# Fixed sizes in place of switches for the experts' second blocks, and a copy moved from GpSimd to ScalarE

## The chip, the cores and the metric

The kernel runs on one core of a Trainium2 chip. The metric is device time in microseconds from the launch to the last output. The core has TensorE (matrix products; PE in the rows, its weight loads PEld), VectorE (DVE), ScalarE (ACT), GpSimd (POOL), and SyncE (SP), which issues most transfers. The engines run side by side, each through its own list of instructions in order, and wait for each other through semaphores. SBUF is the on-chip memory, PSUM the banks that TensorE writes.

## What is computed

The reference chains three layers: a sparse attention over 2 x 768 positions, a routed mixture of eight experts, and a dense layer with a rational activation. The part that the change touches is the second one and the weights of the third:

```python
skip_score = x @ w_skip                       # x: 1536 x 512
xc = x[skip_score > 0]
logits = xc @ w_gate                          # 8 experts
e_idx = np.argmax(logits, axis=1)
for e in range(8):
    mask = e_idx == e
    h = np.maximum(xc[mask] @ w1[e], 0.0)     # 512 -> 1024
    y[mask] = gate_w[mask, None] * (h @ w2[e])
out[do_compute] = xc + y
...
h = x @ w_in                                  # 512 -> 2048
g = P(h) / (Q(h) + 1e-06)                     # P cubic, Q quadratic in |h|
return g @ w_out
```

How many rows an expert gets depends on the inputs. The inputs of the runs are drawn once and stay the same.

## The kernel before

**Attention, routing (up to 96 us).** The attention runs on all engines, and the weights of the first experts are loaded meanwhile. Rows are then sorted by expert: `off` and `end` are an expert's first place and the place behind its last one in the sorted order, `cnt` the difference. `lim` holds the bounds of each block of an expert, `regs` and `pick` hold numbers that engines load into registers.

**Experts (96 to 245 us).** Sorted rows are gathered from DRAM by GpSimd (line 764, `xg`), transposed by TensorE (`turned`, line 1032) and kept as `xs`, rows along the free dimension. An expert's rows are done in two blocks. The first block has up to 32 rows (`SMALL`): `take_first` (VectorE masks and copies the rows into `xw`, lines 864 to 873), `first` (hidden product `th`, line 810), `turn` (`tt`), `parts` (second product `tp`, line 833), `total_first` (`ty`) and `add_first` (VectorE adds the result into `xs`). The second block, the "rest", takes what is left over. Experts 3 to 7 are first reordered by `choose` so that the largest of them stands in slot 3 (`STAY`); only slots 0 to 3 have a rest, and a loop behind `tc.If(left > 0)` (line 1152) takes anything beyond it.

A rest has one of eleven sizes (`ARMS`: 0, 32, 64, 112, 128, 144, 152, 160, 176, 192, 224). VectorE counts which size an expert needs, TensorE and ScalarE load that index (`arms_of`), and `rest` is a `tc.Switch` over eleven written-out arms, with a hint set ahead of it; a switch parts the instruction lists of all engines into blocks. `take_rest` always masks 224 rows (`CAP`), `room` zeroes the whole PSUM tile `py` (line 970), and `update(CAP, ...)` adds 224 columns. The arm of 32 uses the same form as a first block (`thr`, `ttr`, `tpr`, `py`), the arm of 0 nothing, the others `large`: hidden product `phr` (line 783), ScalarE's ReLU `hTr`, second product `py` (line 789).

The weights of experts 3 to 7 are fetched by SyncE (`fetched`, line 1014) into the slots of earlier experts, two matrices of 2 MB each, as soon as TensorE is done with the slot. The order of the whole stage is written out by hand; `turned(4..11)` and `choose` stand behind `rest(0)`; `rest(1)` stands behind `add_first(0)`, `rest(2)` behind `add_first(2)`, `rest(3)` behind `add_first(3)`.

**Decoder.** The dense layer's weights arrive as 64-bit numbers in pieces of 128 x 512. A piece takes three VectorE steps (lines 719, 723, 725, into `dec`, three buffers), then a rounded part `hi` (line 737) and a difference `lo = dec - hi` (line 739). The steps are strewn between the other work by `decoder.steps(fetches, splits)`; half of the 32 pieces are split in the expert stage, half in the last one.

**Dense layer (from 245 us).** 48 rounds, one per 512 rows and 128 hidden units. In each round: product `m` (line 1225), ScalarE's front (lines 1232 to 1234), GpSimd's multiplication `t` (line 1235), ScalarE's logarithm and exponential of the round before (lines 1248, 1249), VectorE's lines 1239 and 1243 and its four steps 1263 to 1268 (`gh`, `u`, `t`, `gl`), and product `z` (line 1283) of two rounds before. Up to three decode steps and three split steps follow VectorE's stages in a round. `split` chooses the engine of `hi`:

```python
if self.on_scalar:
    nc.scalar.activation(hi, src, AF.Copy)
else:
    nc.gpsimd.tensor_scalar(hi, src, 1.0, 0.0, ALU.mult, ALU.add)
yield
nc.gpsimd.tensor_tensor(lo, src, hi.bitcast(F32), ALU.subtract)
```

Of the kernel before, what the change touches and what calls it, by code (L numbers as in the profile page):

```python
# [27 lines left out]
E = 8  # L28
# [41 lines left out]
ARMS = (0, 32, 64, 112, 128, 144, 152, 160, 176, 192, 224)  # L70
# [3 lines left out]
def shape_constants():  # L74
# [27 lines left out]
    ints[:, 305:315] = np.add(ARMS[:-1], 0.5)  # L102
    ints[:, 316:572] = np.arange(256)
    ints[:, 572:604] = np.tile(np.eye(32), (4, 1))
    ints[:, 604:614] = np.add(ARMS[:-1], 0.5)
# [4 lines left out]
def tile_kernel(ctx, tc, q, k, v, w_skip, w_gate, w1, w2, w_in, w_out, pa, pb, ma_d, ints_d, out):  # L110
# [48 lines left out]
    def attention(c, io, wk, ps_s, ps_q, ps_t, ps_o):  # L159
# [468 lines left out]
        for n in range(3):  # L628
# [13 lines left out]
        flag = const.tile([P, E, len(ARMS) - 1], F32, name="flag")  # L642
        nc.vector.tensor_copy(rf[:, 0:9], pb_)
        off, end = rf[:, 0:8], rf[:, 1:9]
        cnt, arm, win, most, fst, sec = (rf[:, 16 + 8 * i : 24 + 8 * i] for i in range(6))
# [3 lines left out]
        nc.vector.tensor_scalar(win, sec, float(N - CAP), None, ALU.min)  # L649
# [4 lines left out]
        nc.vector.tensor_tensor(  # L654
            flag[:],
            lim[:, 3, :, None].to_broadcast(flag.shape),
            ints[:, None, 305:315].to_broadcast(flag.shape),
            ALU.is_gt,
        )
        nc.vector.tensor_tensor(lim[:, 1, :], end, fst, ALU.subtract)  # L660
        nc.vector.tensor_reduce(arm, flag[:], AX.X, ALU.add)
        nc.vector.tensor_tensor(lim[:, 2, :], sec, win, ALU.subtract)
        nc.vector.tensor_copy(regs[:, 8:16], arm[0:1])
        nc.vector.tensor_copy(regs[:, 0:8], win[0:1])
        nc.vector.tensor_copy(regs[:, 40:48], fst[0:1])
        routed.extend([(off, end, cnt), rf[:, 24:40]])
# [91 lines left out]
    with ExitStack() as s_:  # L758
# [97 lines left out]
        def reg(eng, i, top):  # L856
            return eng.value_load(i if not isinstance(i, int) else regs[:, i : i + 1], min_val=0, max_val=top)
# [23 lines left out]
        arms = {}  # L881

        def arms_of(e, which):


            engs = {ET.PE: nc.tensor, ET.Activation: nc.scalar}
            index = {et: reg(eng, which, len(ARMS) - 1) for et, eng in engs.items()}
            arms[e] = index, tc.switch_hint(index, len(ARMS), f"rest{e}")

        def choose():  # L890
# [7 lines left out]
            def t_(name, shape, dt=F32):  # L898
# [4 lines left out]
            left, flag2, win = t_("left", [E]), t_("flag2", [len(ARMS) - 1]), t_("winx", [1])  # L903
# [24 lines left out]
            nc.vector.tensor_scalar(win[:], off2[:, 0:1], float(SMALL), float(N - CAP), ALU.add, ALU.min)  # L928
# [9 lines left out]
            nc.vector.tensor_scalar(more[:, :STAY], off[:, :STAY], float(SMALL + CAP), None, ALU.add)  # L938
            nc.vector.tensor_scalar(more[:, late], off2, float(SMALL), None, ALU.add)
            nc.vector.tensor_scalar(  # L940
                more[:, STAY : STAY + 1], more[:, STAY : STAY + 1], float(CAP), None, ALU.add
            )
# [10 lines left out]
        small, xr, py_first, py_rest, off_first, off_rest = [], {}, {}, {}, {}, {}  # L953
# [22 lines left out]
        def rest(e):  # L976
            a, b_ = wts[e, 1], wts[e, 2]
            py = py_rest[e]
            index, hint = arms[e]
            for i in tc.Switch(index, len(ARMS), hint=hint):  # L980
                n = ARMS[i]
                if n == SMALL:
                    sm = Small(a, b_, xr[e], f"r{e}", ps_h)
                    for step in (sm.hidden, sm.turn, sm.parts):
                        step()
                    sm.total(py, 2)
                elif n:
                    large(a, b_, n, xr[e], py, f"r{e}_{i}")
            update(CAP, off_rest[e], py)
# [60 lines left out]
        with tc.manual_schedule(engines={ET.PE, ET.Activation, ET.DVE, ET.Pool, ET.SP}):  # L1050
# [11 lines left out]
            arms_of(0, 8)  # L1062
            first(0)
            take_rest(0)
            room(0)
# [6 lines left out]
            rest(0)  # L1072
            room(1)
# [21 lines left out]
            arms_of(1, 9)  # L1095
# [9 lines left out]
            room(2)  # L1105
# [4 lines left out]
            arms_of(2, 10)  # L1110
# [11 lines left out]
            room(3)  # L1122
            take_rest(3)
            fetched(5, 4)
            arms_of(3, pick[:, 0:1])
# [64 lines left out]
    with ExitStack() as s_:  # L1190
# [214 lines left out]
```

## Time and profile before

| | value |
|---|---|
| time, median of 3 runs | 557.14 us (554.82 to 558.86) |
| profiled execution | 556.66 us, span 554.9 us |
| busy: TensorE | 466.9 us (84% of the span) |
| busy: VectorE | 409.5 us (74%) |
| busy: ScalarE | 238.6 us (43%) |
| busy: GpSimd | 198.3 us (36%) |
| mean granted TensorE clock | 0.932 of full speed |

The shares are means over stages with different limits, so they name no bound by themselves. The expert stage lies between 96 and 245 us, the dense layer behind it. In the rows below an engine's idle time stands in brackets with what ended it; "issue" means that the engine waited for nothing that the profile shows.

### The profile page before, as it was taken

The page shows a single profiled execution, that of the slowest core. Times are in us where ns is not written, and L with a number is a line of the kernel's source. Part 1 is how long each engine was busy: PE and PEld are TensorE (multiplying, and loading weights), DVE is VectorE, ACT ScalarE, POOL GpSimd, SP SyncE. Part 2 cuts the span into 40 slices and gives each one's busy share as a digit, 9 for nine tenths or more (in the row PEclk, how much of TensorE's full clock was granted, in tenths as well). Part 3 has the DMA queues.
Part 4 walks back from the last instruction along what each step waited for, and adds up shares of the span by engine and source line. Part 5 has one row for each costly group of instructions (what it writes and reads, how often), then busy time and mean ns, then how long its engine had stood idle before and what let it go on. Part 6 is the DMA issues. An engine that isn't in the chain of part 4 may idle for free.

```text
span 554.9 us, 8712 instructions
## 1 busy us (share of the span) xinstructions
PE 466.9 (84%) x3127; PEld 348.3 (63%) x3127; DVE 409.5 (74%) x879; ACT 238.6 (43%) x455; POOL 198.3 (36%) x192
## 2 busy tenths in 40 slices
PE   8999998567868655787977787888999999999994
PEld 4677675344828422345756666567888887888872
DVE  4687678445984231858999999998787797887784
ACT  3565553131112010126444444626565676465650
POOL 2644400710345001635544444644322243322222
PEclk9999998678979887958999999989999999999998
DMA  9799971686393899222222222101000000100001
GB/s 288 219 370 353 402 234 73 183 284 217 133 342 107 292 322 377 85 80 76 76 76 77 76 77 76 38 2 58 20 0 1 0 2 38 38 1 0 2 0 76
DMA packets 28781, 71.67 MB, mean 129 GB/s; under 512 B 3040, under 2 KB 7072, under 8 KB 28704
## 3 DMA queue, kind: packets, MB, share of 16 engines
q1 hardware_dynamic: 24192, 55.26, 28.3%
q0 software_dynamic: 4368, 15.21, 8.1%
q8 instruction: 37, 0.61, 0.4%
q14 instruction: 40, 0.33, 0.2%
q10 hardware_dynamic: 144, 0.27, 0.1%
HBM read 64.44 MB, written 6.29 MB: 127 GB/s over the span
## 4 chain that ended last, share of the span: by engine, by line
PE 18%; DVE 17%; issue 13%; POOL 5%; ACT 2%; POOLq 0%; DVEq 0%; ACTq 0%
PE m L1225 10%; PE z L1283 8%; POOL t L1235 3%; DVE u L1264 2%; DVE t L1267 2%; DVE gh L1263 2%; DVE decwo L719 2%; DVE t L1239 2%; DVE decwi L719 2%; DVE decwi L723 1%; POOL out_dram L1308 1%; DVE decwo L725 1%; DVE gl L1268 1%; DVE decwo L723 1%; DVE decwi L725 1%
## 5 line engine op out<-in xcount | busy, mean ns | idle before, releaser
L1225 PE MATMUL m<-x,wi 128*128 128x512 f32 x576 | 146.2, 405 | 28.5 <-DVE gl L1268 25.9
L1225 PEld LDWEIGHTS m<-x,wi 128*128 128x128 f32 x576 | 110.5, 195 | 59.2 <-DVE gl L1268 29.7
L1235 POOL TENSOR_TENSOR t<-s,t 128x512 f32<-128x512 f32 x48 | 63.3, 1318 | 171.2 <-ACT s L1234 167.8
L1283 PE MATMUL z<-wo,gh 128*128 128x512 f32 x384 | 96.1, 389 | 0.0
L1232 ACT ACTIVATE t<-m,ab 128x512 f32<-128x512 f32 x48 | 37.4, 780 | 113.3 <-PE m L1225 113.3
L1283 PEld LDWEIGHTS z<-wo,gh 128*128 128x128 f32 x384 | 71.9, 188 | 15.2 <-POOL wo L739 0.3
L1283 PE MATMUL z<-wo,gl 128*128 128x512 f32 x192 | 52.6, 391 | 1.1 <-DVE gl L1268 1.1
L1263 DVE SCALAR_TENSOR_TENSOR gh<-t,ab,m 128x512 fp32r<-128x512 f32 (+1 forms) x51 | 36.4, 713 | 17.1 <-ACT m L1249 17.0
L1264 DVE SCALAR_TENSOR_TENSOR u<-t,c,gh 128x512 f32<-128x512 f32 (+1 forms) x51 | 39.3, 770 | 5.5 <-DVE gh L1263 0.5
L1283 PEld LDWEIGHTS z<-wo,gl 128*128 128x128 f32 x192 | 36.0, 188 | 9.8 <-DVE gl L1268 2.3
L1234 ACT ACTIVATE s<-t,absb 128x512 f32<-128x512 f32 x48 | 39.1, 815 | 4.4
L810 PE MATMUL th<-w,xw 128*32 128x256 f32 x256 | 24.2, 548 | 19.3 <-issue 11.1
L1267 DVE SCALAR_TENSOR_TENSOR t<-t,ab,u 128x512 f32<-128x512 f32 (+1 forms) x51 | 36.5, 716 | 1.8
L1239 DVE TENSOR_TENSOR t<-t,m 128x512 f32<-128x512 f32 x48 | 32.8, 684 | 6.1 <-ACT t L1233 5.1
L1268 DVE TENSOR_TENSOR gl<-t,m 128x512 fp32r<-128x512 f32 (+1 forms) x51 | 33.5, 656 | 4.8
L1243 DVE SCALAR_TENSOR_TENSOR t<-t,ab,m 128x512 f32<-128x512 f32 x48 | 35.8, 746 | 1.2
L299 ACT ACTIVATE tm<-tm,mx 128x120 f32<-128x120 f32 x96 | 29.9, 383 | 10.1 <-DVE mx L283 10.0
L1248 ACT ACTIVATE m<-t,c 128x512 f32<-128x512 f32 x48 | 32.3, 672 | 0.2 <-POOL t L1235 0.2
L810 PEld LDWEIGHTS th<-w,xw 128*32 128x32 f32 x256 | 11.3, 150 | 30.3 <-issue 19.2
L283 DVE CUSTOM_DVE_ANT_0 tm<-s,ma 128x120 f32<-128x120 f32 x96 | 21.3, 278 | 11.7 <-PE s L269 11.7
L1249 ACT ACTIVATE m<-m 128x512 f32<-128x512 f32 x48 | 27.9, 582 | 1.5
L1233 ACT ACTIVATE t<-m 128x512 f32<-128x512 f32 x48 | 28.4, 591 | 0.0
(217 smaller groups left out, 728.7 us busy)
## 6 DMA issues: line engine op xcount, KB each, us to landing
w<-in_moe_w_dram SPq DMA_DIRECT2D x16, 2048.0 KB, 11.1
rawwi<-in_moe_w_in_dram POOLq DMA_DIRECT2D x9, 512.0 KB, 4.8
rawwo<-in_moe_w_out_dram POOLq DMA_DIRECT2D x8, 512.0 KB, 4.0
rawwo<-in_moe_w_out_dram SPq DMA_DIRECT2D x8, 512.0 KB, 3.2
rawwi<-in_moe_w_in_dram SPq DMA_DIRECT2D x7, 512.0 KB, 3.5
kT<-in_k_dram SPq DMA_DIRECT2D x8, 400.0 KB, 6.6
ve<-in_v_dram SPq DMA_DIRECT2D x4, 780.0 KB, 7.1
qT<-in_q_dram SPq DMA_DIRECT2D x8, 384.0 KB, 7.9
```

Of the source, the lines that this page charges most:

```text
L810: nc.tensor.matmul(ph[SMALL * g : SMALL * g + SMALL], self.xw[:, c_, :SMALL], self.a[:, c_, 256 * g : 256 * g + 256], start=c_ == 0, stop= ...
L1225: nc.tensor.matmul(ph[:], w[:, l, c_, fs], x[c_][:, r], start=i == 0, stop=i == 3 * KC - 1)
L1232: nc.scalar.activation(t["t2"][:], ph[:], AF.Identity, scale=ab[:, 3:4], bias=ab[:, 2:3])
L1234: nc.scalar.activation(t["s2"][:], t["t1"][:], AF.Identity, scale=absb[:, 1:2], bias=absb[:, 0:1])
L1235: nc.gpsimd.tensor_tensor(t["t1"][:], t["s2"][:], t["t1"][:], ALU.mult)
L1239: nc.vector.tensor_tensor(t["t2"][:], t["t2"][:], ph[:], ALU.mult)
L1243: nc.vector.scalar_tensor_tensor(t["t2"][:], t["t2"][:], ab[:, 1:2], ph[:], ALU.add, ALU.mult)
L1263: nc.vector.scalar_tensor_tensor(gh[:, s], t2[:, s], ab[:, 0:1], r0[:, s], ALU.add, ALU.mult)
L1264: nc.vector.scalar_tensor_tensor(u[:, s], t1[:, s], c1[:, 0:1], gh[:, s].bitcast(F32), ALU.add, ALU.mult)
L1267: nc.vector.scalar_tensor_tensor(t2[:, s], t2[:, s], ab[:, 0:1], u[:, s], ALU.add, ALU.subtract)
L1268: nc.vector.tensor_tensor(gl[:, s], t2[:, s], r0[:, s], ALU.mult)
L1283: nc.tensor.matmul(zs[s4][:], l[:, P * s4 : P * s4 + P], w[:, r, f % 4, :], start=i == 0 and n in starts, stop=i == 2 and n in ends,)
```

## The change

Two things change. First, the eleven sizes and their switches go: each rest has one fixed size from a table `REST`, 0 for expert 0, 128 for expert 1, 160 for expert 2 and 32 for slot 3. With them go the index (three operations of VectorE for experts 0 to 2, three for slot 3, and the register loads on TensorE and ScalarE), the hints, `room` with its zeroing, and for expert 0 the whole rest. `take_rest` and `update` now work on the rest's size instead of 224 rows. The table also enters the constants (`ints`), from which the last place of a rest and the place behind it are computed. Second, in the rounds of the dense layer `decoder.steps` is called with `on_scalar=True`, so sixteen `hi` copies move from GpSimd to ScalarE. The splits in the expert stage stay on GpSimd.

```diff
-ARMS = (0, 32, 64, 112, 128, 144, 152, 160, 176, 192, 224)
+REST = (0, 128, 160, 32, 0, 0, 0, 0)
...
-    ints[:, 305:315] = np.add(ARMS[:-1], 0.5)
+    ints[:, 305:313] = np.subtract(N, REST)
...
-    ints[:, 604:614] = np.add(ARMS[:-1], 0.5)
+    ints[:, 604:612] = np.add(SMALL, REST)
...
-        nc.vector.tensor_scalar(win, sec, float(N - CAP), None, ALU.min)
+        nc.vector.tensor_tensor(win, sec, ints[:, 305:313], ALU.min)
...
-            nc.vector.tensor_scalar(flag2[:], late_ints[:, 288:298], lim[:, 3, STAY : STAY + 1], None, ALU.is_lt)
-            nc.vector.tensor_reduce(best[:], flag2[:], AX.X, ALU.add)
-            nc.vector.tensor_copy(pick[:, 0:1], best[0:1])
...
         def take_rest(e):
+            n = REST[e]
             xr[e] = mw.tile([P, KC, CAP], F32, tag="xr", name=f"xr{e}", bufs=2)
-            off = off_rest[e] = reg(nc.vector, pick[:, 1:2] if e == STAY else e, N - CAP) if e else SMALL
+            off = off_rest[e] = reg(nc.vector, pick[:, 1:2] if e == STAY else e, N - n) if e else SMALL
             lo, hi = lim[:, 2, e : e + 1], lim[:, 3, e : e + 1]
-            gated(masked(CAP, off, lo, hi, f"r{e}"), xr[e])
-
-        def room(e):
-
-            py_rest[e] = ps_y.tile([P, KC, 256], F32, tag="y", name=f"py{e}")
-            nc.vector.memset(py_rest[e][:], 0.0)
+            gated(masked(n, off, lo, hi, f"r{e}"), xr[e])
...
         def rest(e):
-            a, b_ = wts[e, 1], wts[e, 2]
-            py = py_rest[e]
-            index, hint = arms[e]
-            for i in tc.Switch(index, len(ARMS), hint=hint):
-                n = ARMS[i]
-                if n == SMALL:
-                    sm = Small(a, b_, xr[e], f"r{e}", ps_h)
-                    for step in (sm.hidden, sm.turn, sm.parts):
-                        step()
-                    sm.total(py, 2)
-                elif n:
-                    large(a, b_, n, xr[e], py, f"r{e}_{i}")
-            update(CAP, off_rest[e], py)
+            n = REST[e]
+            py = ps_y.tile([P, KC, 256], F32, tag="y", name=f"py{e}")
+            if n == SMALL:
+                sm = Small(wts[e, 1], wts[e, 2], xr[e], f"r{e}", ps_h)
+                for step in (sm.hidden, sm.turn, sm.parts):
+                    step()
+                sm.total(py, 2)
+            else:
+                large(wts[e, 1], wts[e, 2], n, xr[e], py, f"r{e}")
+            update(n, off_rest[e], py)
...
-            arms_of(0, 8)
             first(0)
-            take_rest(0)
-            room(0)
...
-            rest(0)
-            room(1)
...
-                decoder.steps(*k)
+                decoder.steps(*k, on_scalar=True)
```

TensorE's list between the first block of expert 3 and the first block of expert 4, around rest 2, before the change (`tp3` and `th4` are products of those first blocks; `py2`, `hTr2` belong to rest 2, and the arm shown is the one of 32 rows, the first written out):

```order
L833 MATMUL tp3_3815<-w2_3_2649,hT43_3808 32x512 x8
L1401 SWITCH_STRIDE
L1401 ISA x2
L980 BRANCH_PREFETCH_HINT
L1401 UNCONDITIONAL_BRANCH
L980 BRANCH_PREFETCH_HINT
```

And with the change:

```order
L825 MATMUL tp3_2236<-w2_3_1828,hT43_2229 32x512 x8
L775 MATMUL phr2_0_2269<-xr2_1975,w1_2_1151 128x160 x4
L775 MATMUL phr2_1_2275<-xr2_1975,w1_2_1151 128x160 x4
L775 MATMUL phr2_2_2281<-xr2_1975,w1_2_1151 128x160 x4
L775 MATMUL phr2_3_2287<-xr2_1975,w1_2_1151 128x160 x4
L775 MATMUL phr2_4_2293<-xr2_1975,w1_2_1151 128x160 x4
L775 MATMUL phr2_5_2299<-xr2_1975,w1_2_1151 128x160 x4
L775 MATMUL phr2_6_2305<-xr2_1975,w1_2_1151 128x160 x4
L775 MATMUL phr2_7_2311<-xr2_1975,w1_2_1151 128x160 x4
L781 MATMUL py2_2267<-hTr2_2268,w2_2_1273 128x160 x32
L802 MATMUL th4_2377<-w1_4_2111,xw_1649 32x256 x16
```

The switch, the hints and the branches are gone from the list, and rest 2 stands as straight code of 160 columns between the two products. It is the same at rests 1 and 3; rest 0 leaves nothing behind.

ScalarE's list in one round of the dense layer, before the change (`t28`, `t18`, `s28` are the front of round 8, `m7` the logarithm and exponential of round 7):

```order
L1232 ACTIVATE t28_7246<-m8_7231,ab_73 128x512
L1233 ACTIVATE t18_7245<-m8_7231 128x512
L1234 ACTIVATE s28_7244<-t18_7245,absb_6862 128x512
L1248 ACTIVATE m7_7179<-t17_7193,c1_6864 128x512
L1249 ACTIVATE m7_7179<-m7_7179 128x512
L1232 ACTIVATE t29_7297<-m9_7282,ab_73 128x512
```

And with the change, rounds 7 and 8 (`wi3` is the rounded part, `decwi31` the decoded piece):

```order
L1193 ACTIVATE t27_4163<-m7_4148,ab_73 128x512
L1194 ACTIVATE t17_4162<-m7_4148 128x512
L1195 ACTIVATE s27_4161<-t17_4162,absb_3831 128x512
L1209 ACTIVATE m6_4097<-t16_4111,c1_3833 128x512
L1210 ACTIVATE m6_4097<-m6_4097 128x512
L727 ACTIVATE wi3_4171<-decwi31_4174 128x512
L1193 ACTIVATE t28_4215<-m8_4200,ab_73 128x512
```

The copy stands behind the exponential of the round before and ahead of the next round's front. On GpSimd the multiplication and the subtraction now follow each other with nothing between them.

## Rows read from the trace of the kernel before

**Rows 1.** Windows: stretch, length; busy us (instructions) of PE, PEld, DVE, ACT, POOL; clock, DMA share, GB/s
```profile
150.87:185.71 34.84, 26.82 (x204) 20.41 (x204) 19.51 (x32) 4.61 (x13) 14.67 (x17) 0.90 0.62 220
156.00:160.00 4.00, 3.52 (x30) 1.68 (x34) 2.66 (x9) 0.38 (x1) 0.80 (x1) 0.50 1.01 383
185.71:245.10 59.39, 35.08 (x286) 16.51 (x286) 26.21 (x32) 6.82 (x15) 16.89 (x20) 0.76 0.71 257
```

**Rows 2.** Timeline, TensorE around rest 0: start, duration, operation [idle before <-releaser]
```profile
112.91 1.94 PE L1032 MATMUL xsT<-ident,xg 128*128 128x128 f32 x8 [4.68 <-issue]
...
121.07 2.10 PE L1032 MATMUL xsT<-ident,xg 128*128 128x128 f32 x16
127.42 5.35 PE L810 MATMUL th<-w,xw 128*32 128x256 f32 x64 [4.25 <-DVE xw L873]
```

**Rows 3.** Timeline, VectorE ahead of expert 1's first rows
```profile
123.05 0.23 DVE L933 TENSOR_SCALAR flag<-late_ints,lim 128x10 f32<-128x10 f32 x1
...
123.59 0.67 DVE L1038 COPY xs<-xsT 128x512 f32<-128x512 f32 x1
```

**Rows 4.** Timeline, TensorE around rests 1, 2 and 3
```profile
143.56 7.31 PE L789 MATMUL py<-hTr,w 128*128 128x112 f32 x64
156.49 0.69 PE L825 MATMUL tt<-ident,h 128*128 128x128 f32 x2 [5.62 <-issue]
157.10 3.64 PE L810 MATMUL th<-w,xw 128*32 128x256 f32 x32
...
168.92 8.52 PE L783 MATMUL phr<-xr,w 128*128 128x152 f32 x64 [1.98 <-issue]
177.28 8.43 PE L789 MATMUL py<-hTr,w 128*128 128x152 f32 x64
191.22 3.64 PE L810 MATMUL th<-w,xw 128*32 128x256 f32 x32 [5.51 <-issue]
...
202.81 3.56 PE L810 MATMUL thr<-w,xr 128*32 128x256 f32 x32 [3.84 <-issue]
...
217.11 3.23 PE L810 MATMUL th<-w,xw 128*32 128x256 f32 x32 [5.56 <-issue]
...
223.61 1.91 PE L810 MATMUL th<-w,xw 128*32 128x256 f32 x32
```

**Rows 5.** Timeline, TensorE behind the branch for leftovers (line 1152)
```profile
232.55 2.82 PE L810 MATMUL th<-w,xw 128*32 128x256 f32 x32 [3.69 <-PEq L1152]
...
238.23 3.64 PE L833 MATMUL tp<-w,hT 128*32 128x512 f32 x16 [0.54 <-ACT hT L827]
```

**Rows 6.** Timeline of SyncE's queue, then windows: transfers for experts 5 to 7
```profile
182.12 0.38 SPq L1014 DMA_DIRECT2D w<-in_moe_w_dram  x1
...
182.12:222.00 39.88, 21.60 (x182) 11.73 (x184) 10.88 (x16) 3.49 (x8) 2.58 (x4) 0.79 0.94 344
204.00:220.00 16.00, 8.69 (x82) 4.07 (x74) 1.09 (x1) 1.36 (x3) 0.00 (x0) 0.72 1.03 393
```

**Rows 7.** Timeline, one round of the last stage: ScalarE, GpSimd, VectorE; the next round's line 1235
```profile
308.43 1.35 POOL L1235 TENSOR_TENSOR t<-s,t 128x512 f32<-128x512 f32 x1 [3.84 <-ACT s L1234]
308.97 0.58 ACT L1249 ACTIVATE m<-m 128x512 f32<-128x512 f32 x1
309.75 0.62 POOL L737 TENSOR_SCALAR wi<-decwi 128x512 fp32r<-128x512 f32 x1
310.45 1.29 POOL L739 TENSOR_TENSOR wi<-decwi,wi 128x512 fp32r<-128x512 f32 x1
310.75 1.54 DVE L719 SCALAR_TENSOR_TENSOR decwo<-rawwo,low 128x512 int32<-128x512 int32 x1
...
315.60 1.33 POOL L1235 TENSOR_TENSOR t<-s,t 128x512 f32<-128x512 f32 x1 [3.85 <-ACT s L1234]
```

**Rows 8.** Single lines: ns of one, shortest/median/longest; first and last start
```profile
L719 DVE SCALAR_TENSOR_TENSOR decwi<-rawwi,low x16: 684/688/1789, 131.2 to 303.6; 128x512 int32<-128x512 int32 x16
L1212 ACT ACTIVATE x<-xs x12: 612/633/637, 245.2 to 445.9; 128x512 fp32r<-128x512 f32 x12
```

More of the change, by code (lines that the diff above doesn't have):

```diff
@@ L641, in attention @@
         rf = const.tile([P, 72], F32, name="rf")
-        flag = const.tile([P, E, len(ARMS) - 1], F32, name="flag")
         nc.vector.tensor_copy(rf[:, 0:9], pb_)
         off, end = rf[:, 0:8], rf[:, 1:9]
-        cnt, arm, win, most, fst, sec = (rf[:, 16 + 8 * i : 24 + 8 * i] for i in range(6))
+        cnt, _, win, _, fst, sec = (rf[:, 16 + 8 * i : 24 + 8 * i] for i in range(6))
         nc.vector.tensor_tensor(cnt, end, off, ALU.subtract)
         nc.vector.tensor_scalar(sec, off, float(SMALL), None, ALU.add)
-        nc.vector.tensor_scalar(win, sec, float(N - CAP), None, ALU.min)
+        nc.vector.tensor_tensor(win, sec, ints[:, 305:313], ALU.min)
         nc.vector.tensor_scalar(fst, off, float(N - SMALL), None, ALU.min)
@@ L653, in attention @@
         nc.vector.tensor_scalar(gate_s[:], pg[:], 1.0 / 16384.0, None, ALU.mult)
[L654 to L659, printed above, removed]
         nc.vector.tensor_tensor(lim[:, 1, :], end, fst, ALU.subtract)
-        nc.vector.tensor_reduce(arm, flag[:], AX.X, ALU.add)
         nc.vector.tensor_tensor(lim[:, 2, :], sec, win, ALU.subtract)
-        nc.vector.tensor_copy(regs[:, 8:16], arm[0:1])
         nc.vector.tensor_copy(regs[:, 0:8], win[0:1])
         nc.vector.tensor_copy(regs[:, 40:48], fst[0:1])
-        routed.extend([(off, end, cnt), rf[:, 24:40]])
+        routed.append((off, end, cnt))
     with ExitStack() as s_:
@@ L879, in update @@
             nc.vector.tensor_tensor(xs[:, :, win], py[:, :, :n], xs[:, :, win], ALU.add)
[L881 to L888, printed above, removed]
         def choose():
@@ L902, in choose @@
             table, new, step, each = t_("table", [3, n]), t_("new", [3, n]), t_("step", [3, n - 1]), t_("each", [3, n])
-            left, flag2, win = t_("left", [E]), t_("flag2", [len(ARMS) - 1]), t_("winx", [1])
+            left, win = t_("left", [E]), t_("winx", [1])
             number = late_ints[:, STAY:E]
@@ L926, in choose @@
             yield
-            nc.vector.tensor_scalar(win[:], off2[:, 0:1], float(SMALL), float(N - CAP), ALU.add, ALU.min)
+            nc.vector.tensor_scalar(win[:], off2[:, 0:1], float(SMALL), float(N - REST[STAY]), ALU.add, ALU.min)
             nc.vector.tensor_copy(pick[:, 1:2], win[0:1])
@@ L932, in choose @@
             nc.vector.tensor_tensor(lim[:, 3, STAY : STAY + 1], end2[:, 0:1], win[:], ALU.subtract)
-            nc.vector.tensor_scalar(flag2[:], late_ints[:, 288:298], lim[:, 3, STAY : STAY + 1], None, ALU.is_lt)
-            nc.vector.tensor_reduce(best[:], flag2[:], AX.X, ALU.add)
-            nc.vector.tensor_copy(pick[:, 0:1], best[0:1])
             yield
[L938 to L942, printed above, removed]
+            done = late_ints[:, 288 : 288 + E]
+            nc.vector.tensor_tensor(more[:, :STAY], off[:, :STAY], done[:, :STAY], ALU.add)
+            nc.vector.tensor_tensor(more[:, late], off2, done[:, late], ALU.add)
             nc.vector.tensor_copy(ends[:, :STAY], end[:, :STAY])
@@ L952, in tile_kernel @@
         xw = mw.tile([P, E, KC, SMALL], F32, name="xw")
-        small, xr, py_first, py_rest, off_first, off_rest = [], {}, {}, {}, {}, {}
+        small, xr, py_first, off_first, off_rest = [], {}, {}, {}, {}
         def take_first(e):
@@ L1093, in tile_kernel @@
             decoder.steps(*STEPS[0])
-            arms_of(1, 9)
             first(2)
@@ L1104, in tile_kernel @@
             rest(1)
-            room(2)
             fetched(4, 2)
@@ L1109, in tile_kernel @@
             decoder.steps(*STEPS[2])
-            arms_of(2, 10)
             small[2].turn()
@@ L1121, in tile_kernel @@
             rest(2)
-            room(3)
             take_rest(3)
             fetched(5, 4)
-            arms_of(3, pick[:, 0:1])
             first(4)
```

## The prediction

> **What bounds the kernel now.** I read the profile by stage first, then the chain that ends each stretch of the two stages that the change touches.
>
> The expert stage (96 to 245 us) is bound by nothing that is busy. In its last 59 us TensorE works 35 us and VectorE 26 us, at a granted clock of 0.76 [rows 1]. Single instructions of TensorE say why. Around every rest it stands idle with "issue" as the cause, so no semaphore holds it: 4.68 us after rest 0, which has no work at all [rows 2], 5.62 us after rest 1, 1.98 us ahead of rest 2 and 5.51 us behind it, 3.84 us ahead of rest 3 and 5.56 us behind it [rows 4]. These six places are the borders of the four switches; inside a rest and between two rests the rows follow each other closely. The idle time sums to 27.2 us. Behind it TensorE pays again: the hidden product of an expert's first 32 rows takes 3.64, 3.64, 3.56 and 3.23 us right after a gap, and 1.91 us at 223.61 where it follows other work [rows 4]. The granted clock from 156 to 160 us, right behind a gap, is 0.50 [rows 1], the lower of its two levels (1.2 GHz, against 2.4).
>
> The last stage has two halves. While pieces of the weights are still decoded, VectorE is the bound, in rounds of 315.60 - 308.43 = 7.17 us [rows 7]; once the last piece is done, TensorE's products follow each other, and the change touches nothing there. Only the first half can gain.
>
> **Which arms ran.** The sizes in the rows tell what the four rests had to hold: no product between the transposes ahead of the gap and those behind it for rest 0 [rows 2], columns of 112 for rest 1 and 152 for rest 2, and the 32-row form for rest 3 [rows 4]. The fixed sizes 0, 128, 160, 32 cover all four, so the loop for leftovers should stay untaken.
>
> **Rest 0.** Branch, gap and the work on an empty rest go. Transposes that began at 112.91 can follow at once: 4.68 us [rows 2]. VectorE's chain to the first rows of expert 1 loses three small operations for the switch index, from 123.05 to the copy at 123.59: 0.54 us [rows 3]. TensorE then has no gap to fall to the low clock in: eight transposes took 1.94 us behind the gap, sixteen took 2.10 us at full clock [rows 2], some 0.9 us. Of these 6.1 us I expect 5.5, since the transposes also wait for the copies that empty their banks. Bounds: 3.5 (TensorE waits for the gathered rows or the copies instead) and 6.5.
>
> **Rests 1 and 2 become wider.** 112 columns become 128, 152 become 160. The second product took 7.31 us with 112 columns and 8.43 us with 152 [rows 4]: 0.028 us a column, 0.056 for both products. So rest 1 costs 0.9 us more and rest 2 0.45 us. Bounds: 0 (the weight load sets the pace of the narrower one) and twice that.
>
> **From rest 1's end (150.87) to rest 2's end (185.71), 34.84 us.** Both gaps go: 5.62 + 1.98. The product at 157.10 runs at full clock: 3.64 - 1.91 = 1.73. Minus 0.45 for the width: 8.9 us gained [rows 4]. VectorE does 19.5 us of work here [rows 1], within the 25.9 us that stay, and nothing of TensorE in this stretch waits for its decoding: the transposes of a first block wait for ScalarE alone.
>
> **From rest 2's end, call it T, to the stage's end, 59.39 us** [rows 1]. Three gaps, 5.51 + 3.84 + 5.56 = 14.9; three products at full clock, 1.73 + 1.65 + 1.32 = 4.7: 19.6 us. So the first product of expert 5, which ended at T + 34.6, ends at T + 15.0; what follows it stays, the branch for the leftovers with its 3.69 us too [rows 5].
>
> That is where transfers become the cover that could run out. Between 182.12, when expert 5's first matrix is issued, and 222 the engines moved 344 GB/s for 39.88 us, 13.7 MB: the weights of experts 5, 6 and 7 and two pieces for the decoder [rows 6]. At the 393 GB/s of the busiest 16 us [rows 6] the same bytes take 34.9 us. Issued from T - 3.6, as before, they end at T + 31.3. Expert 7's second matrix is first used 238.23 - 220.34 = 17.9 us after expert 5's first product [rows 4, 5], so at T + 32.9. It fits by 1.6 us. Expert 7's first matrix, 2.1 MB earlier, is there at T + 26.0 and wanted 12.2 us after that product [rows 5], at T + 27.2. Because the slack is so thin I take 18.0 of the 19.6. Bounds: 14 (transfers 5 us late) and 21 (the first matrix of expert 5 issued already after rest 2's hidden half, which the order of the change allows).
>
> **ScalarE rounds in the last stage.** Sixteen pieces: two in the first round, then one a round. ScalarE's copy of that shape takes 0.63 us [rows 8] against 0.62 on GpSimd [rows 7]. What it is worth hangs on one stall: VectorE's first decode step (line 719) takes 1.54 us in a round and 0.69 when alone, and it starts inside GpSimd's subtraction (line 739, 310.45 to 311.74) and ends 0.55 us after it [rows 7, 8]. The subtraction needs the rounded part. On ScalarE that comes after the exponential that ends at 309.55, so it is ready at about 310.2; on GpSimd it was ready at 310.37. The subtraction moves by 0.2 us, still into the decode step. And because GpSimd's place in a round is set by the round before, the 0.2 us shows only every other round: 14 rounds x 0.1 to 0.2, I take 1.5 us. Bounds: a loss of 1.3 (the first round's two copies stand ahead of ScalarE's next front, 2 x 0.63) and a gain of 11.9 (14 x 0.85, no stall at all).
>
> The Trainium skill (SBUF — State Buffer, SBUF: two separate sides) says that a VectorE operation with two SBUF inputs and a GpSimd operation that reads SBUF take one port pair by turns, the later one standing still for the whole instruction. By that rule 0.62 us less GpSimd work a piece would be worth up to 14 x 0.62 = 8.7 us; by the rows it is 1.5, since the subtraction that does the blocking stays on GpSimd.
>
> **Sum.** 5.5 - 0.9 + 8.9 + 18.0 + 1.5 = 33.0 us. The profiled execution took 556.66 us (span 554.9), half a microsecond under the median of the runs, 557.14. 556.7 - 33.0 = 523.7 us. The likeliest case alone reaches from 519 to 528.
>
> **Rivals.**
> Transfers give part of it back: at the mean 344 GB/s of rows 6 instead of 393 the 13.7 MB end at T + 36.3, 3.4 us late, and the idle TensorE drops its clock again for another 1.7. For it: experts 5 to 7 already fill the queues from 184 on. Against: the pieces of the decoder are few there. 529 us (526 to 534).
> The stall of the decode step vanishes: the freed GpSimd gets its subtraction done before VectorE arrives. It would have to end 1 us earlier; its multiplication ends at 309.78 and the subtraction needs 1.29 more, to 311.07, past 310.75 [rows 7]. 11.9 instead of 1.5: 513 us. The Trainium skill's rule above (SBUF — State Buffer, SBUF: two separate sides) allows it where the subtraction comes first.
> The gaps are not the branches' but TensorE's own supply of instructions, and stay in straight code. Against: between the gaps the same products run without them [rows 4]. Rest 0, the decode shift and little else would remain: 550 us.
> Slower: an expert outgrows its fixed size and the leftover loop runs. It reloads all eight experts, 16 x 2.1 MB at 393 GB/s = 85 us: above 600 us. It decides at one row over 32 + 0, 128, 160 or 32; the arms that ran exclude it.
>
> **Chances.** Forecast 0.69, transfers late 0.15, stall gone 0.07, gaps stay 0.06, loop 0.02, other 0.01. 515 to 531 takes the first, most of the second and leaves out about 2 in 10 with the tails. One per cent is about what a measurement of this kernel can tell from no change. Faster by over 1%: all but the loop and half of the gaps' case, 0.95; within 1%: 0.03; slower: 0.02.
>
> **What would show it.** Right: no idle "issue" above 2 us on TensorE between the first transposes and the leftover branch; first products near 1.9 us; first product of expert 1 near 122 us, rest 2's end near 172, the last stage's first product near 214; rounds of 7.0 us with the first decode step still around 1.3 us. Wrong: TensorE waiting for a weight's transfer before expert 6 or 7; a decode step at 0.7 us in every round; any row of the leftover loop.

## The result, and the profile after

The changed kernel took 523.2 us (median of four runs, 522.4 to 523.7) against 557.1: a ratio of 0.943, 95% interval 0.938 to 0.948. The profiled execution took 522.7 us with a span of 520.9. 523.7 was forecast, 515 to 531 as the range. So the total came out; some of the terms below it did not, and the experiments are about that. Ratios take a kernel's runs up to 1.5% above its fastest; of the 23 runs of the kernel before beside e9 to e12 that leaves 11, with a median of 555.8 us against 557.0 for all.

TensorE's timeline of the changed kernel through the expert stage (start, duration, operation, [idle before <- what ended it]):

```profile
106.31 2.10 PE L1003 MATMUL xsT<-ident,xg 128*128 128x128 f32 x16
...
112.70 1.53 PE L1003 MATMUL xsT<-ident,xg 128*128 128x128 f32 x12
...
118.22 5.35 PE L802 MATMUL th<-w,xw 128*32 128x256 f32 x64 [2.03 <-DVE xw L865]
...
133.51 7.31 PE L781 MATMUL py<-hTr,w 128*128 128x128 f32 x64
140.97 1.93 PE L802 MATMUL th<-w,xw 128*32 128x256 f32 x32
...
157.30 8.86 PE L781 MATMUL py<-hTr,w 128*128 128x160 f32 x64
166.09 1.93 PE L802 MATMUL th<-w,xw 128*32 128x256 f32 x32
171.24 1.91 PE L802 MATMUL thr<-w,xr 128*32 128x256 f32 x32
178.33 1.93 PE L802 MATMUL th<-w,xw 128*32 128x256 f32 x32
184.66 1.93 PE L802 MATMUL th<-w,xw 128*32 128x256 f32 x32 [0.93 <-DMA w<-in_moe_w_dram]
190.03 2.49 PE L825 MATMUL tp<-w,hT 128*32 128x512 f32 x16 [2.50 <-SPq L1113]
198.28 3.49 PE L802 MATMUL th<-w,xw 128*32 128x256 f32 x32 [5.75 <-SPq L1113]
206.41 3.64 PE L825 MATMUL tp<-w,hT 128*32 128x512 f32 x16 [3.37 <-SPq L1113]
213.87 10.64 PE L1186 MATMUL m<-x,wi 128*128 128x512 f32 x36 [1.14 <-issue]
```

Against [rows 2, 4, 5] one sees three things. No "issue" gap is left between the transposes and 184 us, and the products of 32 first rows up to there take 1.91 to 1.93 us. From 184 on new gaps stand there: 0.93, 2.50, 5.75 and 3.37 us, on expert 6's first product and its second (tp) and on expert 7's first and second. "SPq L1113" is SyncE at the branch for leftovers; I read it as SyncE seeing the weights' transfers land, since without that branch the gaps of expert 7 stand at the same times and are put down to the transfers themselves (e5, below). And behind the new gaps the products are slow again, 3.49 and 3.64 us. In windows (columns as in [rows 1]) the granted clock falls to the lower level in one of these gaps while the DMA engines are full (second row); the third row lies ahead of T, the end of rest 2, and is used further down:

```profile
166.16:213.87 47.71, 30.36 (x286) 13.90 (x287) 20.69 (x32) 7.55 (x17) 18.70 (x22) 0.80 0.81 305
192.00:197.00 5.00, 0.52 (x4) 0.00 (x0) 2.09 (x3) 0.60 (x1) 2.70 (x4) 0.50 1.02 399
150.00:157.50 7.50, 7.50 (x57) 7.50 (x57) 7.16 (x12) 2.08 (x7) 3.01 (x4) 1.00 0.49 164
```

The decoding rounds of the last stage took 6.95 and 7.08 us by turns (starts of GpSimd's multiplication), against 7.17 [rows 7]. Two of them (ScalarE's rounding, GpSimd's subtraction, VectorE's first decode step, now line 711):

```profile
277.29 0.62 ACT L727 ACTIVATE wi<-decwi 128x512 fp32r<-128x512 f32 x1
277.99 1.29 POOL L731 TENSOR_TENSOR wi<-decwi,wi 128x512 fp32r<-128x512 f32 x1 [0.45 <-DVE gl L1229]
278.50 1.34 DVE L711 SCALAR_TENSOR_TENSOR decwo<-rawwo,low 128x512 int32<-128x512 int32 x1
...
284.37 0.62 ACT L727 ACTIVATE wo<-decwo 128x512 fp32r<-128x512 f32 x1
285.07 1.30 POOL L731 TENSOR_TENSOR wo<-decwo,wo 128x512 fp32r<-128x512 f32 x1 [0.45 <-ACT wo L727]
285.43 1.48 DVE L711 SCALAR_TENSOR_TENSOR decwo<-rawwo,low 128x512 int32<-128x512 int32 x1
```

The decode step still starts inside the subtraction and ends some 0.55 us after it.

By the prediction's own stretches (spans 554.9 and 520.9, so 34.0 us to explain):

| stretch | before | after | gained | predicted |
|---|---|---|---|---|
| start to expert 1's first product | 127.42 | 118.22 | 9.2 | 5.5 |
| to rest 1's end | 23.45 | 22.60 | 0.85 | -0.9 |
| to rest 2's end, T | 34.84 | 25.34 | 9.5 | 8.9 |
| T to the last stage's first product | 60.20 | 47.71 | 12.5 | 18.0 |
| the last stage | 309.0 | 307.0 | 2.0 | 1.5 |

### The profile page after: what moved, and what is told of

Its sections match the earlier page's. It is cut to its first block, busy times and chain, and to the rows that moved or that the text cites. A ratio compares the mean times of both kernels' runs of the same rounds, so it can differ in the third digit from the quotient of the medians.

```text
span 520.9 us, 8568 instructions
## 1 busy us (share of the span) xinstructions
PE 457.9 (88%) x3127; PEld 344.4 (66%) x3127; DVE 393.3 (76%) x864; ACT 247.7 (48%) x472; POOL 186.1 (36%) x175
## 4 chain that ended last, share of the span: by engine, by line
DVE 19%; PE 19%; issue 14%; POOL 5%; ACT 2%; POOLq 0%; DVEq 0%; ACTq 0%
PE m L1186 9%; PE z L1244 8%; POOL t L1196 3%; DVE u L1225 3%; DVE t L1228 2%; DVE gh L1224 2%; DVE decwo L711 2%; DVE t L1200 2%; DVE decwi L711 2%; DVE decwi L715 1%; DVE decwo L717 1%; DVE decwi L717 1%; DVE decwo L715 1%; POOL out_dram L1269 1%; DVE gl L1229 1%
## 5 line engine op out<-in xcount | busy, mean ns | idle before, releaser
L1224 DVE SCALAR_TENSOR_TENSOR gh<-t,ab,m 128x512 fp32r<-128x512 f32 (+1 forms) x51 | 36.4, 713 | 17.3 <-ACT m L1210 17.3
L1225 DVE SCALAR_TENSOR_TENSOR u<-t,c,gh 128x512 f32<-128x512 f32 (+1 forms) x51 | 37.6, 737 | 5.1
L802 PE MATMUL th<-w,xw 128*32 128x256 f32 x256 | 19.9, 469 | 8.7 <-SPq L1113 5.8
L270 PE MATMUL s<-kW,qT 64*64 64x120 f32 x384 | 25.1, 272 | 0.0
```

Source lines behind the costliest of these rows:

```text
L1224: nc.vector.scalar_tensor_tensor(gh[:, s], t2[:, s], ab[:, 0:1], r0[:, s], ALU.add, ALU.mult)
L1225: nc.vector.scalar_tensor_tensor(u[:, s], t1[:, s], c1[:, 0:1], gh[:, s].bitcast(F32), ALU.add, ALU.mult)
```

## Experiments

Ratios are to the kernel before on the same chip in the same session; the lengths of stretches are from each kernel's one profiled execution.

### The last stage alone, and the rests alone (e1, e2)

```
e1, in the kernel before:       -decoder.steps(*k)   +decoder.steps(*k, on_scalar=True)
e2, in the changed kernel:      -decoder.steps(*k, on_scalar=True)   +decoder.steps(*k)
```

> The kernel before with one part of the change alone: ScalarE rounds the pieces in the last stage, the four switches stay. The theory (the subtraction that blocks VectorE stays on GpSimd and moves only a little): 1.5 to 2.5 us faster, all of it in the last stage, the first decode step around 1.3 to 1.4 us instead of 1.54, the expert stage as before. Rival one (0.62 us less of GpSimd's work a round is worth that much to VectorE): up to 8.7 us. Rival two (the last stage's gain in the changed kernel came from its other start, not from ScalarE): 0 us.

> The changed kernel without its ScalarE part: rests without switches, GpSimd rounds. The theory that the two parts add up: 32 us faster than before, 525 us, with the expert stage of the changed kernel row for row and the last stage 2 us longer than there. Rival (the two parts share a resource): more than 3 us away from that.

Measured: e1 560.2 us, ratio 1.000 (0.997 to 1.003). e2 525.3 us, ratio 0.940 (0.937 to 0.943). The rests are the whole of what the totals can tell. e2's expert stage is not row for row that of the changed kernel: expert 1's first product starts at 122.44 us, 4.2 us later, behind a standstill that the last section shows. The length of the last stage tells the small part better than the total does. With GpSimd rounding it was 309.0 (before), 308.3 (e2), and 308.6 and 308.2 in two kernels below. With ScalarE it was 307.0 and, in six kernels below that leave the last stage as it is in the changed one (e4 to e9), 307.0 to 307.7. That is about 1 us, between the theory and rival two. In e1 it was 310.2: the rounds did alternate between 6.8 and 7.2 us, but the last four with decoding took 36.1 us together (343.38 to 379.48) where before has 34.5 (344.17 to 378.68). Why, no row tells.

### The blocked decode step (e3)

```
-scalar_tensor_tensor(t, w[:, :, 1], 3, low, logical_shift_left, bitwise_and)
+tensor_scalar(t, w[:, :, 1], 5, 2, logical_shift_left, logical_shift_right)
```

> The changed kernel with the first decode step written as two shifts, by 5 to the left and by 2 to the right, which gives the same bits as shift and mask, and reads one SBUF operand instead of two. The theory (in the last stage VectorE's first decode step stands still beside GpSimd's subtraction because it reads two SBUF operands): the step falls from 1.27 to 1.41 us to some 0.7 in every round, the second step gets a small wait of 0.1 us or so, 14 pieces x 0.55 = 8 us less, about 515 us. Rival one (any VectorE instruction on SBUF stands still beside GpSimd): the step stays at 1.3 us and the time at 523. Rival two (the step gets short, but the rounds are bound by something else): step 0.7 and the time still 521 to 523.

Measured: 522.9 us, ratio 0.935 (0.932 to 0.937), against 525.3 of e2, which also rounds on GpSimd, in the same session; its last stage is 305.5 us long, 1.5 us shorter than the changed kernel's. The step did not fall to 0.7. Two rounds, and the line's summary (ns of one: shortest/median/longest):

```profile
292.80 1.28 POOL L731 TENSOR_TENSOR wo<-decwo,wo 128x512 fp32r<-128x512 f32 x1 [0.45 <-DVE gl L1229]
293.25 1.11 DVE L711 TENSOR_SCALAR decwo<-rawwo 128x512 int32<-128x512 int32 x1
...
299.83 1.29 POOL L731 TENSOR_TENSOR wo<-decwo,wo 128x512 fp32r<-128x512 f32 x1 [0.45 <-ACT wo L727]
299.97 1.44 DVE L711 TENSOR_SCALAR decwo<-rawwo 128x512 int32<-128x512 int32 x1
...
L711 DVE TENSOR_SCALAR decwo<-rawwo x11: 414/1106/1457, 199.7 to 330.7; 128x512 int32<-128x512 int32 x11
```

Alone the two shifts take 0.41 to 0.43 us, where the step with two operands takes 0.68. Beside the subtraction they take 1.11 and 1.44 in these two rounds and end 0.28 us behind it. So my theory that the second SBUF operand is what blocks fell, and rival one held for this form: it is faster alone and blocked all the same. What is won is that the step runs 0.27 us less once it is let go, of which the rounds (6.72 and 7.04 us by turns) keep about half. The Trainium skill (SBUF — State Buffer, Who interferes with whom) has both cases: a VectorE operation with two SBUF inputs beside a GpSimd instruction that reads SBUF, or a one-input operation such as tensor_scalar in a mode that uses both ports, is held for the whole of the GpSimd instruction if that came first. The trace agrees, with 0.41 us alone and 1.11 to 1.44 beside it; that the 0.41 us is such a mode is inferred from its being so much shorter. Whether a VectorE operation with one SBUF input outside such a mode would go free beside GpSimd was not tried.

### What the end of the expert stage waits for (e4, e5, e6)

e4 cuts the bytes that travel beside the weights, e5 takes the branch away, e6 does both.

```
e4, e6: -self.eng.dma_start(raw[:], piece[1])
        +n = 64 if 9 <= self.loads < 17 else 512
        +self.eng.dma_start(raw[:, :n], piece[1][:, :n])    (decoded as eight copies)
e5, e6: -with tc.If(left > 0): ...
```

> The changed kernel with eight of the raw pieces for the decoder (those asked for from 161 us to the end of the expert stage) loaded to an eighth; the decoder reads that eighth eight times, so these parts of the second pair of weights are wrong and every operation keeps its place. That takes 8 x 0.46 = 3.7 MB from the queues beside the weights of experts 5 to 7. The theory (behind rest 2 the stage waits for bytes, and more pieces travel there than was counted): at 390 GB/s these are 9.4 us, so expert 6's second and expert 7's two matrices arrive up to 9 us earlier, the stretch from rest 2's end to the last stage's first product falls from 47.7 to about 40.5, and the whole to about 516. Rival (the branch for the leftovers and the decoder's chain set that stretch's end): under 2 us gained.

> The changed kernel without the loop for leftovers and its branch (left out: that loop, which no row of these inputs enters). The theory (behind rest 2 the stage's end waits for the weights of experts 6 and 7 to land): expert 7's matrices land when they did, TensorE's 5.75 us in front of expert 7's hidden product stay nearly whole as a wait for a transfer, and the time falls by 0 to 1.5 us. Rival (the branch itself sets that gap): 3.5 us or more gained.

> The kernel with eight raw pieces cut to an eighth (second pair of weights partly wrong) and without the loop for leftovers as well. The theory (with the bytes gone the stretch behind rest 2 is bound by TensorE's own chain and the branch): the branch's gap of 4.8 us in front of expert 7 goes, 3.5 to 4.5 us less than with the short pieces alone, about 515.5. Rival (transfers still bind there): under 1 us less.

Measured: e4 519.3 us, ratio 0.928 (0.925 to 0.930). e5 520.0 us (519.0 to 523.5), ratio 0.933 (0.928 to 0.937). e6 515.6 us, ratio 0.926 (0.921 to 0.931). From T to the last stage's first product: e4 38.4 us, e5 48.8, e6 39.5, against 47.7. These lengths can't be compared as they stand, since T moves too: it is at 173.1 us in e4, 165.2 in e5, 167.3 in e6 and 166.2 in the changed kernel, and a late T alone makes the stretch short (41.4 us in e2, with all bytes and T at 171.3). Nearest to like with like are e6 and e7 (all bytes, and the branch), with T at 167.25 and 167.27: the last stage begins at 206.73 and at 214.56, 7.8 us apart, and expert 7's second matrix, the last to be issued, lands at 198.9 and at 207.7 (the last issue plus the longest time to landing). e6, then e7:

```profile
L991 SPq DMA_DIRECT2D w<-in_moe_w_dram x10: 372/380/3897, 111.1 to 178.4; - x10
...
DMA to landing us min/median/max: 7.9/12.6/20.5
```

```profile
L985 SPq DMA_DIRECT2D w<-in_moe_w_dram x10: 372/380/6895, 111.9 to 181.4; - x10
...
DMA to landing us min/median/max: 9.8/14.5/26.3
...
214.56 10.28 PE L1186 MATMUL m<-x,wi 128*128 128x512 f32 x36 [1.14 <-issue]
```

Leaving out the branch alone moved neither in e5's profiled execution (206.4 and 213.97 us, against 206.2 and 213.87 in the changed kernel). So the bytes set when the weights land, and the end of the stage with it. On the whole time they are worth 3.6 to 6.0 us with the branch in place (e4 against e3 and e2 of its session, whose last stages differ by 1 to 2 us from e4's), more than the rival's 2. Expert 7's two products on TensorE's timeline in e5, and its first one in e4 and in e6:

```profile
198.54 3.54 PE L802 MATMUL th<-w,xw 128*32 128x256 f32 x32 [3.90 <-DMA w<-in_moe_w_dram]
...
206.46 3.64 PE L825 MATMUL tp<-w,hT 128*32 128x512 f32 x16 [3.11 <-DMA w<-in_moe_w_dram]
```

```profile
200.58 3.64 PE L808 MATMUL th<-w,xw 128*32 128x256 f32 x32 [4.80 <-PEq L1119]
```

```profile
193.47 2.87 PE L808 MATMUL th<-w,xw 128*32 128x256 f32 x32 [3.52 <-DMA w<-in_moe_w_dram]
...
206.73 10.59 PE L1165 MATMUL m<-x,wi 128*128 128x512 f32 x36 [1.20 <-ACT x L1152]
```

In e5 expert 7's products start at 198.54 and 206.46, in the changed kernel at 198.28 and 206.41: the gaps stay and are now named as transfers. In e4, with the bytes gone, it is the branch that TensorE stands at (its sequencer, PEq, 4.80 us); in e6, with both gone, it is a transfer again, a sooner one. Counted from T, expert 7 starts after 32.1 us in the changed kernel, 33.4 in e5, 27.4 in e4 and 26.2 in e6: branch and transfer lie over each other, and the transfer is the longer of the two as long as all bytes travel in the old order. The median of e5 is 2.8 us under e7's in the same session, between the theory's 1.5 and the rival's 3.5. Its profiled execution took 523.1 us, 3 us more than its median, so the rows above can't show where that gain comes from; what the branch is worth on the whole time stays open. So it does between e4 and e6: 3.7 us by the medians of two chips, 0.9 by the ratios.

What travels there, from the DMA views of before (182 to 222 us) and of the changed kernel (157.50 to 206.40): packets and bytes, then issues of one kind, KB each and median us to landing.

```profile
DMA packets 4976, 13.73 MB, mean 343 GB/s; under 512 B 123, under 2 KB 123, under 8 KB 4964
...
q0 software_dynamic: 288, 1.05, 6.7%
...
w<-in_moe_w_dram SPq DMA_DIRECT2D x6, 2048.0 KB, 11.1
```

```profile
DMA packets 5973, 17.28 MB, mean 353 GB/s; under 512 B 240, under 2 KB 240, under 8 KB 5960
...
q0 software_dynamic: 1256, 4.56, 24.6%
...
w<-in_moe_w_dram SPq DMA_DIRECT2D x6, 2048.0 KB, 17.4
```

The same six matrices, and 4.56 MB of the decoder's pieces (GpSimd's queue, q0) in place of 1.05. The mean rate didn't fall; the load rose, and a matrix lands 17.4 us after its issue instead of 11.1. Not all of that is the pieces': in e4, with 0.39 MB of them from 164.5 to 204 us, the median is still 14.3 us. The six matrices are issued within 23.1 us in the changed kernel and 19.8 in e4, within 29.5 before, so they also stand behind each other.

### Narrower rests (e7)

```
-REST = (0, 128, 160, 32, 0, 0, 0, 0)   +REST = (0, 112, 152, 32, 0, 0, 0, 0)
```

> The changed kernel with rests of 112 and 152 columns in place of 128 and 160. If columns cost alike everywhere: 0.9 us less in rest 1 and 0.45 us less in rest 2. By the rows of the changed kernel (second product 7.31 us with 112 columns and with 128, 8.43 with 152 and 8.86 with 160): 0 in rest 1, 0.4 us a product and 0.9 in all in rest 2. On the whole time, under both, less than 1 us, since transfers set the end of the stage.

Measured: 522.9 us, ratio 0.938 (0.933 to 0.943). The second products of rests 1 and 2:

```profile
135.48 7.31 PE L781 MATMUL py<-hTr,w 128*128 128x112 f32 x64
...
158.84 8.43 PE L781 MATMUL py<-hTr,w 128*128 128x152 f32 x64
```

112 columns cost what 128 cost, 7.31 us; 152 cost 0.43 less than 160. The stretch from rest 1's end to T is 0.86 us shorter, and the last stage began at 214.56 us, no sooner than in the changed kernel. That alone doesn't tell what sets the end: expert 1 started 2.4 us later in this execution, and T came 1.1 us later.

### Asking for the weights sooner (e8, e9, e10)

Between 150 and 157.5 us the changed kernel's DMA engines are half idle (164 GB/s, share 0.49, above): expert 5's first matrix waits for expert 2's slot. e8 takes expert 4's first rows ahead of and into rest 2, so that expert 4's slots come free first. e9 is the changed kernel again, e10 is e8 with e3's two shifts.

```
+first(4)
-rest(2)
+rest(2, between)    # between its two products: small[4].turn(), small[4].parts(), fetched(5, 2)
 take_rest(3)
-fetched(5, 4)  first(4) ... small[4].turn() ... small[4].parts()  fetched(6, 2)
+fetched(6, 4)
 decoder's slots: -(6, 4, 2, 0)[G]   +(6, 2, 4, 0)[G]
```

> The changed kernel with expert 4's first rows taken ahead of rest 2 (hidden product) and into its middle (transposes and second product), so that expert 4's two slots are free some 8 us earlier; expert 5's weights go there and expert 6's into expert 2's slots, and the decoder's order of slots follows. The theory (the stretch behind rest 2 waits for bytes, and the queues stand nearly idle from 150 to 157 us): the transfers of experts 5 to 7 start some 7 us sooner and end 6 to 8 us sooner, about 516. Rival one (TensorE now waits for expert 4's weights ahead of rest 2, or the decoder's pieces come late by as much): 521 to 525. Rival two (the end of the stage isn't set by transfers): no change.

> The changed kernel once more, beside the next ones on the same chip: 523 us. Its trace tells whether the first product of expert 1 starts at 118 us or, as in three variants, at 122 to 124, where ScalarE and VectorE stood still for some 4 us ahead of the transposes.

> Expert 4 early (weights asked for sooner) and the first decode step as two shifts together. The theory (one gains in the expert stage, the other in the last stage's decoding half, nothing shared): 5.7 + 1.5 to 2 us less than the changed kernel, about 515.5. Rival (a shorter last stage waits for something that the stage before now leaves late): 517.5 as with expert 4 early alone.

Measured: e8 517.5 us (517.0 to 519.9), ratio 0.930 (0.925 to 0.935). e9 521.8 us, 0.940 (0.934 to 0.945). e10 516.5 us, 0.929 (0.923 to 0.936), 5.3 us under e9 on the same chip. In e9 expert 1 starts at 119.30 us, without the standstill. e8 is 5.3 us under e7, which ran on its chip. e8 in the same idle window, and its TensorE at expert 7 and at the last stage's start:

```profile
150.00:157.50 7.50, 7.47 (x73) 6.54 (x74) 7.02 (x13) 1.60 (x5) 2.59 (x4) 1.00 0.79 285
```

```profile
196.72 3.64 PE L804 MATMUL th<-w,xw 128*32 128x256 f32 x32 [4.98 <-PEq L1118]
203.01 1.92 PE L827 MATMUL tp<-w,hT 128*32 128x512 f32 x16 [1.25 <-SPq L1118]
208.22 11.25 PE L1191 MATMUL m<-x,wi 128*128 128x512 f32 x36 [1.14 <-issue]
```

The theory held for the end of the stage: with all bytes and the branch still there, the last stage begins 5.7 us sooner, at 208.22, and ahead of expert 7 it is now the branch (4.98 us) that is seen. The transfers moved less than was expected: expert 5's first matrix is issued 5.5 us sooner (152.0 against 157.5), the last one lands 3.3 us sooner (202.9 against 206.2, not 6 to 8), and expert 7's second product starts 3.4 us sooner. The other 2.3 us lie behind it, where that product took 1.92 us in place of 3.64. e10's last stage is 305.6 us long, as e3's, but its first product came at 212.56 in an execution of 520.0 us, 3.5 above its median. That median is only 1 us under e8's, from another chip and inside both intervals: whether the two add up is not settled.

### One switch, and the size of a switch (e11, e12)

```
e11: -arms_of(0, 8)   -take_rest(0)   -room(0)   -rest(0)
e12: -ARMS = (0, 32, 64, 112, 128, 144, 152, 160, 176, 192, 224)   +ARMS = (0, 32, 112, 152)
```

> The kernel before with rest 0 alone taken out (its switch, its empty work, its two flags' use; the three other switches stay). The theory (a switch costs its gap, and TensorE's low clock behind it costs as much again): the first product of expert 1 starts 8 to 9 us earlier than before, at 118 to 119 us, and as nothing behind it waits for transfers with three gaps left, the whole falls by 7 to 9 us. Rival one (only the gap and little else, as the prediction had it): 5.5 us. Rival two (the later weights or the decoder take it back): under 3 us.

> The kernel before with four arms in each switch (0, 32, 112 and 152 columns) in place of eleven; the sizes that run are the same. The theory (each border is one jump out of the straight run of instructions, whose price doesn't hang on the number of arms): the six gaps stay at 2.0 to 5.6 us, the time within 3 us of before. Rival (the price is the distance jumped over, or the amount of code loaded): the gaps fall to under half and the time by 10 us or more.

Measured: e11 554.8 us, ratio 1.001 (0.997 to 1.005). e12 558.2 us, ratio 1.007 (1.002 to 1.013). Against the 557.0 us of all runs of the kernel before on that chip, e11 is 2.2 us shorter and e12 1.2 longer. In e11 expert 1's first product starts at 120.61, 6.8 us sooner than in [rows 2], and rest 2 ends 5.4 us sooner; the last stage begins at 245.39, 0.5 us sooner. The place where it is lost, on e11's TensorE:

```profile
185.78 1.08 PE L810 MATMUL th<-w,xw 128*32 128x256 f32 x6 [5.42 <-issue]
190.18 3.62 PE L810 MATMUL th<-w,xw 128*32 128x256 f32 x26 [3.33 <-issue]
```

Expert 4's first product, 3.64 us in one piece behind its gap before [rows 4], has a second "issue" gap of 3.33 us inside. From 186 to 189 us the DMA engines were at 0.9 or more with weights. That the instructions behind the jump came late through the same engines fits, but was not tried apart. Rival two held: one switch taken away alone gives most of its time back downstream.

e12's gaps on TensorE:

```profile
113.79 1.94 PE L1032 MATMUL xsT<-ident,xg 128*128 128x128 f32 x8 [5.08 <-issue]
...
157.25 0.68 PE L825 MATMUL tt<-ident,h 128*128 128x128 f32 x2 [5.36 <-issue]
...
190.71 3.64 PE L810 MATMUL th<-w,xw 128*32 128x256 f32 x32 [5.21 <-DVE xr L873]
...
215.41 3.64 PE L810 MATMUL th<-w,xw 128*32 128x256 f32 x32 [6.05 <-issue]
```

With the two ahead of rests 2 and 3 (1.16 and 2.86 us) the six sum to 25.7 us, against 27.2 with eleven arms. (Two of e12's six are named after VectorE, 5.21 and 2.86 us, but stand at the same borders.) So the price of a switch doesn't hang on its arms, four or eleven. That it is the price of the jumps, and not of loading the index or of the engines' lists being parted there, is argued from where the gaps stand and was not tried apart.

## Why the prediction came out, and where its steps did not

**The bound.** Right: the six gaps were the switches' and went, and the low clock behind them too; the 1.91 us of a first product at full clock, read from one row [rows 4], held wherever TensorE had not waited.

**Rest 0: 5.5 predicted, 9.2 measured**, outside the bounds of 3.5 to 6.5. The working counted the gap, three small operations and 0.9 us of slow transposes. By the rows of both kernels the 9.2 us are the gap, 4.7; some 2.8 from the transposes behind it to the last ones (112.91 to 121.07 before [rows 2], about 107.4, half-way through the sixteen at 106.31, to 112.70 after), in place of the 0.9; 0.8 in VectorE's chain, in place of 0.54; and 0.8 ahead of the gap, which the working didn't have. It left out that everything between 113 and 119 us ran behind that gap: the granted clock there was 0.50 (112.9 to 116 us) and then 0.78 (to 119.2), and the transposes of each block waited a little for the one before. In the session of e1 to e4 it was 6.5 to 8.1 us: starts of 122.4 to 124.0 against 130.6 in e1, which keeps the switches.

**Width: a cost of 1.35 predicted.** What failed in this term is the straight line from 112 to 152 columns, 0.028 us a column. Between 112 and 128 a column costs nothing (e7). Rest 1 cost 0 in place of 0.9, rest 2 0.87 in place of 0.45. That the stretch to rest 1's end even gained 0.85 us is its hidden product, 8.04 us to the second product's start before and 7.24 after, of which 0.56 was a wait for ScalarE. One row each at two widths doesn't tell the form of the curve between them.

**Rest 1's end to T: 8.9 predicted, 9.5 measured.** Right in its parts: both gaps and the slow product went. The width cost 0.4 us more than forecast, and small products behind the gap, not counted, gave 0.8 back.

**T to the stage's end: 18.0 predicted, 12.5 measured**, outside the bounds of 14 to 21. This is the step that failed. The mechanism was named as the thin cover, and the wrong showed as foretold (TensorE waiting for a weight ahead of experts 6 and 7). The transfers were to end at T + 31.3; the last matrix landed at 206.2 us, T + 40.0. Two terms were mis-sized. The bytes: 13.7 MB were carried over from before, with two of the decoder's pieces; in the changed kernel eight travel beside the same six matrices, 17.3 MB in all, and 3.5 MB more at 393 GB/s are 9 us. And the rate: 393 GB/s held only while the engines were full (390 to 414 from 177 to 197 us); over all of these transfers the mean was 353, much as before (about 344), which is another 5 us. The earlier issue (157.50, 8.7 us ahead of T instead of 3.6) gave 5 us back. Without these bytes e6's stretch is 39.5 us, near the 40.6 that the full 19.6 would leave, though e6 lacks the branch too.

**The sum as a whole.** That it came within half a microsecond is luck: the misses cancelled, +3.7, +1.75 and twice half a microsecond on one side, -5.5 on the other. The signs show it: rest 2's end was to be near 172 us and came at 166.2, the last stage near 214 and came at 213.9. And the sum had not seen that its terms are not independent. In the five kernels with all bytes in the old order besides the changed one (e2, e3, e5, e7, e9) T lies between 165.2 and 171.9 us, expert 7's second matrix lands between 206.4 and 209.8, and the last stage begins between 212.7 and 216.1, without following T: e2, with T at 171.3, begins it first. So, as far as one execution of each tells, the end is set by the weights' arrival, and what is gained ahead of T lengthens TensorE's wait. Where T came near the predicted 172 (e2 and e3), the stretch behind it was 41.4 and 44.2 us, gains of 18.8 and 16.0, inside the bounds. So "transfers late", a rival with 0.15, is what happened, at about its price: 5.5 us, against its 3.4 + 1.7. The time is not its 529 us because the other stretches had gained 6.5 more.

**ScalarE's rounding: 1.5 predicted, 2.0 by the spans, 1.0 by the stages' lengths.** Right in mechanism: from 243 us on, the step starts inside the subtraction in twelve rounds of thirteen and takes 1.34 to 1.49 us there. The up to 8.7 us that the prediction worked out by the rule of the Trainium skill (SBUF — State Buffer, SBUF: two separate sides) didn't come, since the work that blocks stayed on GpSimd.

**The gaps as TensorE's own supply** fell: they went with the switches. What a jump costs was read from rows only. The Trainium skill (Runtime: NRT & Kernel Launch, Instruction fetch mechanics) says that a taken branch out of the pages at hand makes the engine wait for the transfer of the target's page. The trace agrees in that the gaps stood at the six borders, 27.2 us, and did not hang on the number of arms; that a transfer of instructions was what TensorE waited for there, no run shows.

## What to carry to other kernels

When a change shortens a stage, count the bytes that will then travel in what is left, other streams' too, instead of carrying the old window's bytes over: the same transfers in a shorter stage are a denser load. Look for the queue's idle time just ahead of the wait; here a first matrix issued 5.5 us sooner was worth more (5.3 us, e8 against e7) than removing the branch beside it (2.8, e5 against e7). And test whether terms add by shifting one of them: an end that doesn't follow when the work before it moves by 6 us is set by something else.

## What the runs showed of the hardware that was not expected

In one session four kernels (e1 to e4), with switches and without, had ScalarE and VectorE standing still some 3.5 to 5 us at about 105 us. ScalarE's relu of expert 0's first rows, in the changed kernel and in e2:

```profile
106.45 0.38 ACT L812 ACTIVATE h<-th 128x256 f32<-128x256 f32 x1 [2.85 <-PE th L802]
```

```profile
109.92 0.38 ACT L812 ACTIVATE h<-th 128x256 f32<-128x256 f32 x1 [6.87 <-remote]
```

Its product had ended at 106.37 and at 105.06. "remote" is something that this core's trace doesn't hold; what it is stays open. It moved expert 1's start by some 4 us; the last stage of e2 and e3 began 1.2 us sooner and 2.3 later than the changed kernel's.

Two shifts with constants take 0.42 us on 128x512 integers where shift and mask with a second operand take 0.68, and both stand still beside a GpSimd subtraction of 1.29 us. And 64 products of 128x112 and of 128x128 columns take the same 7.31 us.
